# Attention and two MoE layers: transposes ahead of a product's last quarter, gate buffers for raw weights, sums behind j9

## The chip, the cores and the metric

The kernel runs on one core of a Trainium2 chip. The metric is device time in microseconds, from the first to the last instruction with the launch around it; the time of a kernel is the median of its runs.

## What is computed

Three layers, one after the other, on a batch of 4 with 8 heads, 576 positions and head dimension 64. All inputs and outputs are float32.

```python
scores = scale * np.matmul(q, k.transpose(0, 1, 3, 2))
bias = np.maximum(x @ w1 + b1, 0.0) @ w2      # x: log distances, 576 x 576
scores = scores + bias.transpose(2, 0, 1)[None, :, :, :]
attn = softmax(scores)
x = np.matmul(attn, v)                        # -> 2304 tokens x 512

h = x @ w_in                                  # first MoE: 512 -> 1024
e = np.exp(h - h.max(-1)); sm = e / (e.sum(-1) + 1e-09)
solu = h * sm
ln = (solu - mean) / np.sqrt(var + 1e-06) * g_ln
x = ln @ w_out                                # 1024 -> 512

gate = 1.0 / (1.0 + np.exp(-(x @ w_gate)))    # second MoE: 512 -> 1536
val = x @ w_val
out = gate * val @ w_out                      # 1536 -> 512
```

## The kernel before

Weights arrive as 64-bit floats, which the kernel reads as pairs of 32-bit words and decodes (`decode`, L184 to L199): two operations on ACT (L191, L192) and two on DVE (L193, L195) per pair of 128-row blocks. Every matrix operand is then split into a high and a low float16 part, and a product is the sum of three matmuls (high x high, high x low, low x high).

**Attention** runs in 72 ticks. A tick computes the scores of a block (`a_qk`, PE, L560 and L565, tile `score`), its softmax on DVE and ACT, a split into float16, a DMA transpose on SP's queue (L608, `pt`), and four ticks later the product with the values (L627, `xps`). K, V and Q arrive by DMA and are transposed on PE (`ktp` L258, `qtp` L297).

**First MoE.** It works by tiles of 128 tokens, 18 of them, as side work in the ticks: `moe_items` (L894) yields small pieces, three of which run in a tick. For tile i these are: `m_g1`, the first product, in four quarters of six matmuls (L773, PSUM tile `hps`, whose eviction with the row maximum is DVE's L784); `m_ew1`, exponential and product; `m_ew2`, mean and variance, ending in POOL's L807, which writes `e`; `m_ew3`, eight PE transposes of `e` (L816, `ltp`), each half of them copied out by ACT (L818) and DVE (L819) into `lt`; `m_g2`, the second product in four parts of 24 matmuls (L830, `x2ps`), which read `lt`, evicted by L835 and L836. `hps`, `ltp` and `x2ps` rotate through the PSUM banks of the pool `ps_m`: three buffers and, in the ticks, a fourth single bank that the class `Turns` (L91) puts at every fourth place. About 13 tiles are done within the attention; the rest follow, with `hps` in the ring `s_ps`.

**Weights of the second MoE.** 18 pairs of 1 MB each (two loads of 512 KB) are loaded by SP through `load_pair` (L1062 to L1071) into the tile `wraw`, for which there are two buffers, one from the end of attention and one from slightly later on; a load waits until the decode of the pair two before is done. ACT's L1148 squares the result for the column scales. `w2_split` (L702 to L706) then scales and splits it: a scaling (L704 on POOL or L702 on ACT, tile `w2tmp`), a copy (L705 on ACT) and the low part (L706 on POOL or DVE).

**Second MoE.** There are five groups of tiles (4, 2, 4, 4, 4). Groups 0 and 1 use `gate_val`: for each of 12 column blocks j, 24 matmuls (L1383) into one of the two buffers of `s_ps`, evicted by ACT's sigmoid (L1388, `fr`), DVE's product (L1389, `fr`) and `split_gv` (L1252 on ACT, L1253 on DVE) into the ring `gv` (two buffers). `second_out` (L1413, `ops`; L1417, `ob`) multiplies by w_out. Groups 2 to 4 use seven products of sums in place of eight (L1347, `prod`); the sums of weights and inputs come from `w2_sums` (six calls of 14 adds, the adds at L1271, tiles `fs` and `w2s`) and `x2_sums` (18 adds per group).

**What sets the order.** The program is written once; a scheduler places each instruction on its engine's queue by dependences and priority. In the attention ticks PE's order is that of the program. Each engine then runs its queue in order. `issue_after` makes a piece wait until a named instruction has issued: the sums of group 2 wait for `glob["so"]`, the last instruction of the scales of w_out.

Of the kernel before, what the change touches and what calls it, by code (L numbers as in the profile page):

```python
# [11 lines left out]
I32 = mybir.dt.int32  # L12
# [78 lines left out]
class Turns:  # L91


    def __init__(self, *pools):
        self.pools, self.n = list(pools), -1

    def tile(self, *a, **kw):
        self.n += 1
# [4 lines left out]
def attn_moe_kernel(  # L103
# [10 lines left out]
    def enter(stack, name, bufs=1, side="left", space=None):  # L114
        kw = {} if space is None else {"space": space}
        if space is None:
            kw["reuse_waits"] = "tile"
            kw["side"] = side
        return stack.enter_context(tc.tile_pool(name=name, bufs=bufs, **kw))
# [9 lines left out]
    att = ctx.enter_context(ExitStack())  # L129

    pss = ctx.enter_context(ExitStack())
    ps_m = Turns(*[enter(pss, "ps_m", 3, space=PSUM)] * 3)
    ps_v = enter(pss, "ps_v", 1, space=PSUM)
    psa = ctx.enter_context(ExitStack())
    ps_s = enter(psa, "ps_b0", 2, space=PSUM)
# [761 lines left out]
    def moe_items():  # L897
        for i in range(19):
            if i < 18:
                for n in range(2):  # L900
                    for half in range(2):
                        yield ready[i] + LAG_PV + LAG_X + 1, (lambda i=i, n=n, half=half: m_g1(i, n, half))
                yield 0, (lambda i=i: m_ew1(i))
            if i >= 1:
                yield 0, (lambda i=i: m_ew3(i - 1))
            if i < 18:
                yield 0, (lambda i=i: m_ew2(i))
            if i >= 1:
                for dc in range(4):
                    yield 0, (lambda i=i, dc=dc: m_g2(i - 1, dc))  # L910
# [149 lines left out]
    w2raw, loads = {}, []  # L1060

    def load_pair(mat, jc, cc):  # L1062
        raw = w2r_p.tile([128, 2, 512, 2], I32, name="wraw", tag="wraw")
        r0 = 256 * cc + (512 * jc if mat == 2 else 0)
        src = (w_gate, w_val, w_out2)[mat]
        cols = slice(0, DM) if mat == 2 else slice(512 * jc, 512 * jc + 512)
        for c in range(2):
            with tc.issue_after(loads[-1].ins):
                loads.append(sp.dma_start(out=raw[:, c].rearrange("p f t -> p (f t)"),
                                          in_=src[r0 + 128 * c:r0 + 128 * c + 128, cols].bitcast(I32)))  # L1070
        return raw  # L1071
# [3 lines left out]
    for t in range(nticks + LAG_PV + LAG_X + 1):  # L1075
        if not own and "open" in done:
            own.append(in_order.enter_context(tc.manual_schedule(engines={mybir.EngineType.PE})))
        with tc.high_priority(PRIO):
            for f in at.get(t, []):
                f()  # L1080
        for u in range(t, t + 3):
            if u < nticks:
                for tt in {0: (), 1: (2, 3), "M": (4,)}[ticks[u][1]]:
                    until(("bias", tt))
                load_bias(ticks[u])
        with tc.high_priority(PRIO):
            if t < nticks:
                a_qk(t)
                a_soft(t)
            if 0 <= t - 1 < nticks:  # L1090
                a_split(t - 1)
            if 0 <= t - LAG_PV - LAG_X < nticks:
                a_x(t - LAG_PV - LAG_X)
        if t % 2 == 0 and 2 <= t < 16:
            with tc.issue_after(trs[t - 1].ins):
                for n in (0, 1) if t == 2 else (t // 2,):
                    store0(n % 2, n // 2)
        for n in range(NB if "s" in glob else NB0):
            side_step(t)
            if n == 0:  # L1100
                with tc.high_priority(PRIO):
                    for f in late.get(t, []):
                        f()
        with tc.high_priority(PRIO):
            if 0 <= t - LAG_PV < nticks:
                a_pv(t - LAG_PV)
            if 0 <= t - LAG_PV - LAG_X < nticks:
                a_xt(t - LAG_PV - LAG_X)
        if t == nticks:
            w2r_p = Turns(enter(glob["s"], "w2e", 1))  # L1110
            loads.append(trs[nticks - 1])
            w2raw[0, 0, 0] = load_pair(0, 0, 0)
    in_order.close()
# [9 lines left out]
    grow("fr", 2, ctx)  # L1123
    d2 = ctx.enter_context(ExitStack())
    w2t_p = enter(d2, "w2t", 2, "right")
    w2r_p.pools.append(enter(d2, "w2r", 1, "right"))
    w2d_p = enter(d2, "w2d", 1, "right")
    w2f = [w2_p.tile([128, 12, 512], F32, name=f"w2f{i}") for i in range(3)]
    w2h16 = [w.bitcast(F16).rearrange("p a (l f) -> p a l f", l=2) for w in w2f]
# [106 lines left out]
        load_x2(0)  # L1236
    glob["s"].close()
    m1.close()
    w2r_p.pools[0] = enter(d2, "w2r2", 1, "right")
    grow("xb", 1, ctx, "left")  # L1240
    grow("gv", 2, ctx, "left")
    grow("fr", 3, ctx, "left")
# [7 lines left out]
    def split_gv(y, gv, js, t0, w):  # L1250
        hi, lo = (gv[:, l, js, t0:t0 + w] for l in range(2))
        act.activation(out=hi, in_=y, func=ACTF.Copy)  # L1252
        dve.tensor_tensor(out=lo, in0=y, in1=hi, op=ALU.subtract)  # L1253

    def half_w(mat, jc, kh, fh):

# [111 lines left out]
    def gate_val(g, n, xx, gvs, js):  # L1368
        nn = 128 * n
        for j in js:  # L1370
# [16 lines left out]
            sg = f32t().rearrange("p j q -> p (j q)")[:, 0:nn]  # L1387
            act.activation(out=sg, in_=prods[0], func=ACTF.Sigmoid, scale=sw[:, j // 4, W_CG:W_CG + 1])  # L1388
            dve.scalar_tensor_tensor(out=sg, in0=prods[1], scalar=2.0 ** -14, in1=sg, op0=ALU.mult, op1=ALU.mult)  # L1389
            split_gv(sg, gv, jj, 0, nn)  # L1390

    def gate_val7(n, xs_, gvs, jcs=range(3)):
        nn = 64 * n
# [50 lines left out]
    with tc.issue_after(glob["so"].ins):  # L1444
        for jc in range(3):
            for mat in range(2):
                w2_sums(mat, jc)
        xs_ = x2_sums(2)
    fring[0] = "fr"
    second_out(1, sizes[1], gvs1)  # L1450
    pss.close()
# [80 lines left out]
```

## Time and profile before

| | |
|---|---|
| median of 3 runs | 1060.28 us (1060.22 to 1061.12) |
| profiled execution, its own time | 1060.07 us |
| its span, first to last instruction | 1058.3 us |
| PE busy | 891.4 us (84%) |
| DVE busy | 732.9 us (69%) |
| ACT busy | 645.0 us (61%) |
| POOL busy | 385.6 us (36%) |
| chain that ended last | PE 35%, DVE 7%, ACT 4%, issue 3% |

The profiled execution has 1.8 us around its span, and it is 0.2 us under the median. Busy shares are means over stages: the attention with most of the first MoE lasts to about 568 us, the rest of the first MoE and the decoding of the second MoE's weights to about 690, and from there the second MoE's matmuls.

### The profile page before, as it was taken

To read this page: it belongs to the slowest core of one execution; us is meant where nothing else is said; L and a number is where in the kernel's file an instruction comes from. 1 tells how busy PE (TensorE), PEld (TensorE's weight loads), DVE (VectorE), ACT (ScalarE), POOL (GpSimd) and SP (SyncE) were. 2 spreads that over 40 slices of the span, in tenths; PEclk is the share of its full clock that TensorE was granted. 3 is DMA by queue.
4 is the path that set the end of the run, shared out by engine and by line. 5 is a ranking of instruction groups with operands and counts; after the bars stand their busy time and mean duration, and the time that the engine had idled before them with its cause. 6 is when DMAs were issued, how large, how long until landed. Compare 5 with 4: busy or idle time off the path is not lost.

```text
span 1058.3 us, 23827 instructions
## 1 busy us (share of the span) xinstructions
PE 891.4 (84%) x9572; PEld 632.2 (60%) x9572; DVE 732.9 (69%) x1471; ACT 645.0 (61%) x1275; POOL 385.6 (36%) x362
## 2 busy tenths in 40 slices
PE   2656563669888889999999888988999999999998
PEld 2634342446656657666766566435578857866873
DVE  6878986696676776576664897699935763871760
ACT  4788877576877788877974888774333322332231
POOL 3357555374666556554550483351000000000000
PEclk9557776679998899999999899898999999999999
DMA  7977999799999699999965655300010010001001
GB/s 224 296 217 192 250 240 242 179 218 215 218 207 197 159 207 189 197 210 201 173 123 163 210 173 200 126 16 35 31 46 16 1 61 21 1 11 31 2 1 40
DMA packets 256575, 146.54 MB, mean 138 GB/s; under 512 B 215376, under 2 KB 230992, under 8 KB 256464
## 3 DMA queue, kind: packets, MB, share of 16 engines
q1 hardware_dynamic: 253168, 141.86, 56.1%
q0 software_dynamic: 2048, 1.58, 0.6%
q8 instruction: 75, 1.23, 0.5%
q10 hardware_dynamic: 1248, 1.57, 0.4%
q14 instruction: 36, 0.29, 0.1%
HBM read 82.46 MB, written 20.05 MB: 97 GB/s over the span
## 4 chain that ended last, share of the span: by engine, by line
PE 35%; DVE 7%; ACT 4%; issue 3%; POOL 1%; DMA 1%; SPq 0%; ACTq 0%; POOLq 0%; DVEq 0%
PE prod L1347 16%; PE ops L1413 12%; PE s_ps L1383 3%; DVE fs L1271 2%; PE x2ps L830 2%; DMA wraw<-in_moe_w_out_dram 1%; PE hps L773 1%; POOL w2tmp L704 1%; DVE w2f L195 1%; DVE w2f L193 1%; ACT wraw L192 1%; DVE w2s L1271 1%; ACT w2junk L1148 1%; PE xps L627 1%; ACT w2f L191 1%
## 5 line engine op out<-in xcount | busy, mean ns | idle before, releaser
L603 POOL TENSOR_TENSOR p<-p,p 128x1024 f16<-128x1024 f32 x72 | 156.7, 2177 | 138.3 <-ACT p L602 93.5
L1271 DVE TENSOR_TENSOR fr<-prod,fr 128x512 f32<-128x512 f32 x126 | 85.0, 687 | 94.3 <-PE prod L1347 92.6
L1413 PE MATMUL ops<-w2f,gv 128*128 128x512 f16 x648 | 142.3, 379 | 0.0
L591 ACT ACTIVATE p<-p,m,sc 128x576 f32<-128x576 f32 x144 | 124.0, 862 | 2.5
L830 PE MATMUL x2ps<-lt,w1f 128*128 128x128 f16 x1728 | 110.2, 223 | 10.0 <-DVE lt L819 7.4
L627 PE MATMUL xps<-gk,pt 128*128 128x64 f16 (+1 forms) x2240 | 85.7, 201 | 35.8 <-DMA pt<-p 29.4
L1383 PE MATMUL s_ps<-xb,w2f 128*128 128x512 f16 (+1 forms) x576 | 103.6, 339 | 14.1 <-DVE fr L1389 11.5
L584 DVE CUSTOM_DVE_ANT_0 p<-score,gk 128x576 f32<-128x576 f32 x144 | 102.9, 751 | 17.7 <-PE score L565 15.0
L830 PEld LDWEIGHTS <-w1f 128*128 128x128 f16 x1728 | 104.2, 100 | 14.4 <-issue 11.6
L627 PEld LDWEIGHTS <-pt 128*128 128x128 f16 (+1 forms) x2240 | 80.5, 106 | 46.3 <-DMA pt<-p 37.3
L1413 PEld LDWEIGHTS <-gv 128*128 128x128 f16 x648 | 63.4, 98 | 73.9
L463 PEld LDWEIGHTS <-mask 128*128 128x128 f16 (+1 forms) x1312 | 64.0, 120 | 48.9 <-issue 26.5
L1347 PEld LDWEIGHTS <-w2f 128*128 128x128 f16 x864 | 84.5, 98 | 11.8 <-issue 1.1
L1383 PEld LDWEIGHTS <-w2f 128*128 128x128 f16 x576 | 58.0, 101 | 55.6 <-issue 13.4
L1252 ACT ACTIVATE gv<-fr 128x512 f16<-128x512 f32 (+1 forms) x60 | 34.7, 585 | 84.2 <-DVE fr L1403 70.4
L560 PE MATMUL score<-gk,qt 64*128 64x512 f16 (+1 forms) x480 | 67.6, 418 | 14.6 <-DVE m L584 11.3
L773 PE MATMUL hps<-w1f,xt 128*128 128x512 f16 x312 | 75.0, 388 | 4.2 <-DVE mm L784 3.6
L463 PE MATMUL bp<-rhs,mask 128*128 128x64 f16 (+1 forms) x960 | 49.2, 222 | 24.2 <-DVE gk L489 6.7
L602 ACT ACTIVATE p<-p 128x1152 f16<-128x1152 f32 x54 | 62.7, 1160 | 11.2 <-DMA pt<-p 8.8
L1347 PEld LDWEIGHTS <-w2s 128*128 128x128 f16 x648 | 63.4, 98 | 7.3
L589 ACT ACTIVATE m<-m,sc 128x1 f32<-128x1 f32 x144 | 39.5, 286 | 44.3 <-DVE m L584 44.2
L773 PEld LDWEIGHTS <-xt 128*128 128x128 f16 x384 | 37.1, 100 | 45.4 <-issue 9.4
(199 smaller groups left out, 1740.7 us busy)
## 6 DMA issues: line engine op xcount, KB each, us to landing
gk<-bias_d SPq DMA_DIRECT2D x24, 576.0 KB
wraw<-in_moe_w_out_dram SPq DMA_DIRECT2D x20, 512.0 KB
wraw<-in_moe_w_gate_dram SPq DMA_DIRECT2D x12, 512.0 KB
wraw<-in_moe_w_val_dram SPq DMA_DIRECT2D x12, 512.0 KB
sraw<-in_q_dram SPq DMA_DIRECT2D x12, 384.0 KB
sraw<-in_k_dram SPq DMA_DIRECT2D x12, 384.0 KB
sraw<-in_v_dram SPq DMA_DIRECT2D x12, 384.0 KB
bias_d<-gk SPq DMA_DIRECT2D x8, 576.0 KB
```

Source lines behind the costliest of these rows:

```text
L463: pe.matmul(big[0:np_, jj // 8, o:o + 64], lhsT, rhs[i].rearrange("p c h g -> p (c h g)"), start=(i == 0), stop=(i == 1),)
L560: pe.matmul(score[p0:p1, 1024 * hh:1024 * hh + 512], qt[rows, nr * ql + r, p0:p1], KT[bb, hp][rows, 640 * kl:640 * kl + 512], start=(m == ...
L584: dve.tensor_tensor_reduce(out=pp[:, hh], in0=score[:, 960 * hh:960 * hh + S], in1=bi, scale=1.0, scalar=-3.0e38, op0=ALU.add, op1=ALU.max ...
L591: act.activation(out=pp[:, hh], in_=pp[:, hh], func=ACTF.Exp, bias=m[:, 2 + hh:3 + hh], scale=col(C), accum_out=sm[:, c + hh:c + hh + 1])
L603: pool.tensor_tensor(out=p16[:, :, 640:1152], in0=view(pp, 0, [[640, 2], [1, 512]]), in1=view(p16, 0, [[1280, 2], [1, 512]]), op=ALU.subtract)
L627: pe.matmul(o, a, b_, start=(n == 0), stop=(n == len(seq) - 1))
L773: pe.matmul(h, xt[:, xl, kk, off:off + 128], win16[:, 2 * kk + n, wl], start=(kk == 0 and xl == 0 and wl == 0), stop=(kk == 3 and xl == 1),)
L830: pe.matmul(ps[:, dc], wout16[:, f, wl, 128 * dc:128 * dc + 128], lt[:, ll, f], start=(n == 0), stop=(n == 23))
L1271: dve.tensor_tensor(out=out_, in0=a, in1=b, op=op)
L1347: pe.matmul(p[:, jf, 0:nn], w(wl, kk, jf), x(xl, kk), start=(m == 0), stop=(m == 5))
L1383: pe.matmul(ps[:, 0:n], w[:, 4 * (j // 4) + c, wl, o:o + 128], xx[:, 0:n, c, xl, :], start=(m == 0), stop=(m == 11))
L1413: pe.matmul(ps, gvs[j // 4][:, gl, j % 4, 128 * tt:128 * tt + 128], w2h16[2][:, j, wl], start=(m == 0), stop=(m == 35))
```

## The change

It has four parts. The turns over the PSUM banks start at another number, so other tiles get the fourth bank. Pairs 1, 2, 5 and 6 of the raw weights are loaded into the two `gv` buffers, which gate_val does not use yet; the others take `wraw`'s two. The sums wait for the low part (L1253's instruction) of j9 of group 0, and `x2_sums(2)` follows the first third of `w2_sums`. In the first MoE, `m_ew3` of the tile before stands ahead of the last quarter of `m_g1`, and `m_ew2` directly behind `m_ew1`.

```diff
 class Turns:
-    def __init__(self, *pools):
-        self.pools, self.n = list(pools), -1
+    def __init__(self, pool):
+        self.pools, self.n = [pool] * 3, 0
...
-    ps_m = Turns(*[enter(pss, "ps_m", 3, space=PSUM)] * 3)
+    ps_m = Turns(enter(pss, "ps_m", 3, space=PSUM))
...
                     for half in range(2):
+                        if n == half == 1 and i >= 1:
+                            yield 0, (lambda i=i: m_ew3(i - 1))
                         yield ready[i] + LAG_PV + LAG_X + 1, (lambda i=i, n=n, half=half: m_g1(i, n, half))
                 yield 0, (lambda i=i: m_ew1(i))
-            if i >= 1:
+                yield 0, (lambda i=i: m_ew2(i))
+            else:
                 yield 0, (lambda i=i: m_ew3(i - 1))
-            if i < 18:
-                yield 0, (lambda i=i: m_ew2(i))
...
     def load_pair(mat, jc, cc):
-        raw = w2r_p.tile([128, 2, 512, 2], I32, name="wraw", tag="wraw")
+        n = len(loads) // 2
+        if n in (1, 2, 5, 6):
+            raw = ring("gv", [128, 2, 512, 2], I32)
+        else:
+            raw = w2r_p[n in (3, 7) or (n > 8 and n % 2)].tile([128, 2, 512, 2], I32, name="wraw", tag="wraw")
...
     def split_gv(y, gv, js, t0, w):
...
-        dve.tensor_tensor(out=lo, in0=y, in1=hi, op=ALU.subtract)
+        return dve.tensor_tensor(out=lo, in0=y, in1=hi, op=ALU.subtract)
...
-            split_gv(sg, gv, jj, 0, nn)
+            low_ = split_gv(sg, gv, jj, 0, nn)
+            if (g, j) == (0, 9):
+                glob["so"] = low_
...
         for jc in range(3):
             for mat in range(2):
                 w2_sums(mat, jc)
-        xs_ = x2_sums(2)
+            if jc == 0:
+                xs_ = x2_sums(2)
```

The order of instructions shows it at three places. The first is PE in the attention, at a tile whose second product follows in the same tick (`ltp` are the transposes, `hps` the first product of the next tile, `x2ps` the second product). Before, the rows were:

```order
L565 LDWEIGHTS qt
L565 MATMUL score<-gk,qt 128x2x64
L816 MATMUL ltp<-id_sb,e 128x128 x8
L297 MATMUL qtp<-id_sb,qraw 128x128 x2
L830 LDWEIGHTS w1f_111
L830 MATMUL x2ps<-lt,w1f_111 128x128
```

and the change has, at that tile:

```order
L773 LDWEIGHTS xt
L773 MATMUL hps<-w1f_110,xt 128x512
L816 MATMUL ltp<-id_sb,e 128x128 x8
L773 LDWEIGHTS xt
L773 MATMUL hps<-w1f_110,xt 128x512
L773 LDWEIGHTS xt
```

The transposes (x8) stood behind the last `hps` and the `score` of the tick, two `qtp` ahead of the first `x2ps`; they now stand between two quarters of `hps`, and the six matmuls of the last quarter, a tick's `xps` and `score` come between them and `x2ps`.

The second is DVE at the end of the decoding (w2f_9631 is w_out's tile, L193 and L195 decode one pair of it; the `fr` are those of j2 and j3, on whose bank j4 waits). Before, three pairs of w_out were decoded ahead of these two `fr` and the next stood behind them:

```order
L195 SCALAR_TENSOR_TENSOR w2f_9631<-wraw,w2f_9631 128x1024
L836 SCALAR_TENSOR_TENSOR x_10612<-x2ps,x_10612 128x4x128
L1389 SCALAR_TENSOR_TENSOR fr<-s_ps,fr 128x512 x2
L706 TENSOR_TENSOR w2f_9629<-w2tmp,w2f_9629 128x512
L193 SCALAR_TENSOR_TENSOR w2f_9631<-w2f_9631,wraw 128x1024
L1253 TENSOR_TENSOR gv<-fr,gv 128x512
L195 SCALAR_TENSOR_TENSOR w2f_9631<-wraw,w2f_9631 128x1024
L1253 TENSOR_TENSOR gv<-fr,gv 128x512
L706 TENSOR_TENSOR w2f_9629<-w2tmp,w2f_9629 128x512
L193 SCALAR_TENSOR_TENSOR w2f_9631<-w2f_9631,wraw 128x1024
L195 SCALAR_TENSOR_TENSOR w2f_9631<-wraw,w2f_9631 128x1024
L1389 SCALAR_TENSOR_TENSOR fr<-s_ps,fr 128x512
```

and now:

```order
L193 SCALAR_TENSOR_TENSOR w2f_9631<-w2f_9631,wraw 128x1024
L195 SCALAR_TENSOR_TENSOR w2f_9631<-wraw,w2f_9631 128x1024
L162 TENSOR_REDUCE acc<-w2st 128x1 x2
L836 SCALAR_TENSOR_TENSOR x_10612<-x2ps,x_10612 128x4x128
L169 TENSOR_SCALAR cl<-tot 128x3
L1258 TENSOR_TENSOR gv<-fr,gv 128x512
L171 TENSOR_SCALAR ci<-cl 128x3
L1258 TENSOR_TENSOR gv<-fr,gv 128x512
L172 TENSOR_SCALAR ci<-ci 128x3
L1394 SCALAR_TENSOR_TENSOR fr<-s_ps,fr 128x512
L173 TENSOR_SCALAR sw<-ci 128x3
L1394 SCALAR_TENSOR_TENSOR fr<-s_ps,fr 128x512
```

All six pairs are ahead of the two `fr` (L1394 in the changed file), with the first steps of w_out's scales (L169 to L173). On SP's queue, the twelve loads of w_out now stand in one row, and the load of `xb` for group 1 behind them.

The third is DVE at the start of the sums (`gv` is the low part's eviction; L1271 is L1276 in the changed file, L1253 is L1258). Before, the sums began with the eviction of j8 still to come:

```order
L1253 TENSOR_TENSOR gv<-fr,gv 128x512
L1177 SCALAR_TENSOR_TENSOR sw<-sw,sc 128x1 x3
L1179 SCALAR_TENSOR_TENSOR sc<-sc 128x1
L1271 TENSOR_TENSOR fs<-w2f_9629 128x512 x3
L1271 TENSOR_TENSOR fs<-fs 128x512
L1271 TENSOR_TENSOR fs<-w2f_9629 128x512
L1389 SCALAR_TENSOR_TENSOR fr<-s_ps,fr 128x512
L1271 TENSOR_TENSOR fs<-fs 128x512
L1271 TENSOR_TENSOR w2s_11685<-fs,w2s_11685 128x512
L1271 TENSOR_TENSOR fs<-fs,w2f_9629 128x512
L1271 TENSOR_TENSOR fs<-w2f_9630 128x512
L1253 TENSOR_TENSOR gv<-fr,gv 128x512
```

and now:

```order
L1394 SCALAR_TENSOR_TENSOR fr<-s_ps,fr 128x512
L1258 TENSOR_TENSOR gv<-fr,gv 128x512
L1394 SCALAR_TENSOR_TENSOR fr<-s_ps,fr 128x512
L1258 TENSOR_TENSOR gv<-fr,gv 128x512
L1394 SCALAR_TENSOR_TENSOR fr<-s_ps,fr 128x512
L1258 TENSOR_TENSOR gv<-fr,gv 128x512
L1276 TENSOR_TENSOR fs<-w2f_9629 128x512 x3
L1276 TENSOR_TENSOR fs<-fs 128x512
L1276 TENSOR_TENSOR fs<-w2f_9629 128x512
L1276 TENSOR_TENSOR w2s_11685<-fs,w2s_11685 128x512
L1276 TENSOR_TENSOR fs<-fs 128x512
L1394 SCALAR_TENSOR_TENSOR fr<-s_ps,fr 128x512
```

The scales that stood directly ahead of the sums are further up, and the `fr` and `gv` of j8 and j9 are ahead of the first sum.

## Rows read from the trace of the kernel before

**Rows 1.** Busy time by stretch: us from:to, length, each engine, PEclk, DMA share, GB/s.

```profile
125.00:150.00 25.00, 14.00 (x211) 11.16 (x211) 19.14 (x46) 18.44 (x38) 15.20 (x15) 0.66 1.09 251
600.00:625.00 25.00, 24.10 (x239) 17.12 (x238) 22.18 (x45) 21.87 (x33) 18.22 (x15) 0.93 0.56 183
700.00:725.00 25.00, 18.10 (x86) 9.24 (x84) 25.00 (x28) 14.84 (x27) 13.12 (x9) 0.86 0.12 42
750.00:775.00 25.00, 25.00 (x175) 16.86 (x174) 21.93 (x39) 11.04 (x21) 0.00 (x0) 1.00 0.06 22
```

**Rows 2.** Chain of waits, 690 to 800: start us, us, what.

```profile
692.16 2.42 DVE fs L1271 x4
...
729.60 0.34 DVE fr L1389
...
729.99 2.78 PE s_ps L1383 x24
...
795.24 0.69 ACT ob L1417
...
795.98 4.09 PE prod L1347 x36
```

**Rows 3.** Waits of PE, 590 to 800: total us, times, longest us.

```profile
PE s_ps L1383 <- DVE fr L1389: 11.5, 3, 4.7
```

**Rows 4.** PE's timeline: start, us, line, operation, count, [idle before <-releaser].

```profile
604.46 2.75 PE L773 MATMUL s_ps<-w1f,xt 128*128 128x512 f16 x12 [0.52 <-DVE mm L784]
...
663.14 23.16 PE L1383 MATMUL s_ps<-xb,w2f 128*128 128x512 f16 x95 [4.64 <-DVE fr L1389]
...
706.08 5.34 PE L1383 MATMUL s_ps<-xb,w2f 128*128 128x512 f16 x24 [2.16 <-DVE fr L1389]
...
718.10 5.07 PE L1383 MATMUL s_ps<-xb,w2f 128*128 128x256 f16 x24 [4.74 <-DVE fr L1389]
```

**Rows 5.** Waits of PE, 250 to 568.

```profile
PE x2ps L830 <- DVE lt L819: 7.0, 8, 1.6
PE ktp L258 <- DMA kv<-in_k_dram: 5.7, 3, 2.9
...
PE ltp L816 <- DVE mm L784: 3.1, 3, 1.8
...
PE x2ps L830 <- ACT lt L818: 1.8, 3, 0.8
```

**Rows 6.** Waits of SP's queue, 555 to 690, then of ACT, 560 to 690.

```profile
SPq L1069 <- DVE w2f L195: 76.5, 15, 7.3
...
ACT w2f L191 <- DMA wraw<-in_moe_w_out_dram: 6.9, 3, 3.0
...
ACT wraw L192 <- DMA wraw<-in_moe_w_gate_dram: 5.0, 1, 5.0
ACT w2f L191 <- DMA wraw<-in_moe_w_gate_dram: 4.1, 1, 4.1
```

**Rows 7.** Groups by line, 560 to 700: busy us, mean ns of one.

```profile
L191 ACT ACTIVATE w2f<-wraw 128x1024 f32<-128x1024 f32 x18 | 20.6, 1144 | 11.7 <-DMA wraw<-in_moe_w_out_dram 6.9 <-DMA wraw<-in_moe_w_gate_dram 4.1 <-DMA wraw<-in_moe_w_val_dram 0.5
...
L192 ACT ACTIVATE wraw<-wraw 128x1024 int32<-128x1024 uint16 x18 | 20.5, 1140 | 5.0 <-DMA wraw<-in_moe_w_gate_dram 5.0
...
L1148 ACT ACTIVATE w2junk<-w2f 128x1024 bf16<-128x1024 f32 x12 | 12.6, 1050 | 3.2 <-DVE w2f L195 3.2
```

**Rows 8.** Timelines of DVE and of POOL, at 706.

```profile
706.55 1.64 DVE L1271 TENSOR_TENSOR fs<-w2f 128x512 f32<-128x512 f16 x1
...
706.08 1.56 POOL L706 TENSOR_TENSOR w2f<-w2tmp,w2f 128x512 f16<-128x512 f32 x1 [3.61 <-ACT w2f L705]
```

**Rows 9.** The page's costliest groups: busy us, mean ns of one | idle before, releaser.

```profile
L1271 DVE TENSOR_TENSOR fr<-prod,fr 128x512 f32<-128x512 f32 x126 | 85.0, 687 | 94.3 <-PE prod L1347 92.6
```

**Rows 10.** Waits of PE, 60 to 250.

```profile
PE xps L627 <- DMA pt<-p: 28.9, 12, 5.2
PE ktp L258 <- DMA kv<-in_k_dram: 9.6, 3, 4.7
```

More of the change, by code (lines that the diff above doesn't have):

```diff
@@ L1109, in attn_moe_kernel @@
         if t == nticks:
-            w2r_p = Turns(enter(glob["s"], "w2e", 1))
+            w2r_p = [enter(glob["s"], "w2e", 1)]
             loads.append(trs[nticks - 1])
@@ L1125, in attn_moe_kernel @@
     w2t_p = enter(d2, "w2t", 2, "right")
-    w2r_p.pools.append(enter(d2, "w2r", 1, "right"))
+    w2r_p.append(enter(d2, "w2r", 1, "right"))
     w2d_p = enter(d2, "w2d", 1, "right")
@@ L1238, in attn_moe_kernel @@
     m1.close()
-    w2r_p.pools[0] = enter(d2, "w2r2", 1, "right")
+    w2r_p[0] = enter(d2, "w2r2", 1, "right")
     grow("xb", 1, ctx, "left")
```

## Prediction

> **What bounds the kernel now.** I read the busy time by stretches first, because the change touches three places with different limits [rows 1]. The columns to look at are PE's busy time, PEclk and the DMA share. From 125 to 150 us PE works 14.00 of 25 us, with the 16 DMA engines full (share 1.09): loads and DMA transposes set that stage. From 600 on PE is nearly full, 24.10 of 25, except where the second MoE starts: in 700:725 it works 18.10 us at clock 0.86 while DVE works 25.00. So DVE leads there, and PE follows.
>
> The chain of waits says the same [rows 2]: from 692.16 to 729.60 its pieces are DVE's, nearly all the sums of L1271, with a `fr` (L1389) between them; at 729.99 it goes over to PE and stays there, and 795.98 is the first seven-product matmul, behind a 0.69 us wait for ACT's `ob`. What follows is dense matmul work that the change leaves alone. So I look for time only ahead of 795.98.
>
> PE's own waits give its size [rows 3]: after 590 the bank evictions `fr` cost it 11.5 us in 3 waits. The timeline [rows 4] places them: 4.64 us before 663.14 (behind the decoding), 2.16 before 706.08 and 4.74 before 718.10 (both behind sums). In the attention stage [rows 5] the second product of the first MoE (`x2ps`) waits for `lt` 7.0 and 1.8 us in eleven waits.
>
> **Transposes a quarter earlier.** No instruction is added or removed: eight transposes, their copies on ACT (L818) and DVE (L819), and the normalisation pass (ew2) move. The eleven waits, 7.0 + 1.8 = 8.8 us, are PE waiting for copies whose transposes it has just done. Now six matmuls of L773 lie between (twelve took 2.75 us [rows 4], so about 1.4 us), and often a whole tick's `xps` and `score` too. The longest such wait is 1.6 us [rows 5], so nearly all 8.8 can go. What is late next: the copies now stand on ACT and DVE ahead of the last quarter's bank evictions (L784), for which `ltp` waits 3.1 us already [rows 5], and PE reaches the k loads (`ktp`, 5.7 us) sooner. Ends: 0 (all of it turns into those waits) and -11.9 (8.8, and the 3.1 of `ltp` too). I take **-5**, a little over half, since the waits on L784 show that this ring is short of banks.
>
> **Four load buffers.** SP's queue waits 76.5 us in 15 waits for the last decoding step (L195) to free a buffer, and ACT waits 6.9 + 4.1 + 5.0 = 16.0 us for the loads that therefore come late [rows 6]. With four buffers for the first eight pairs those 16.0 us can go. But the order puts something in their place: all six pairs of w_out are now decoded, with the squares, ahead of `fr` of j2 and j3, where three of them came after it. Three pairs more on ACT ahead of that point are 3 x (1.144 + 1.140 + 1.050) = 10.0 us [rows 7]; with a fourth square and the readings of the sums of squares that go with them, some 12 us. So the start of j4, now 663.14 [rows 4], moves by +12 less what comes back of 16.0. Ends: +12 (nothing comes back) and -4 (all). I take half, **+4**; the same ACT also waits for POOL and DVE, which more buffers don't shorten.
>
> **Sums after j9.** In the order of before the sums stand on DVE from j8's `fr` on, now from j10's. About seven adds lie between two `fr` either way; what differs is what they meet. Some adds take 1.64 us, beside a POOL split of 1.56 us [rows 8], others 0.6 (four in 2.42 us at 692.16 [rows 2]). With four slow ones in seven a j costs DVE 4 x 1.64 + 3 x 0.6 + 1.3 (`fr` and `gv`) = 9.7 us, and PE needs 5.34 for its 24 matmuls [rows 4]: hence the waits of 2.16 and 4.74. With none it is 7 x 0.6 + 1.3 = 5.5, and PE, which has `ops` of about a microsecond to put between, need not wait. The splits follow the scales of w_out; those come before j4 in the changed order, and the sums start some 35 us after j4 does (six j's of 5.3 and a few `ops`), so the splits should be over. From 663.14 to 795.98 are 132.84 us. Out of these go 2.16 + 4.74 = 6.9, and the slow clock behind the second wait: 24 matmuls of 256 columns took 5.07 us at 718.10 (1.2 GHz) and 2.78 at 729.99 (2.4 GHz) [rows 2, 4], 2.3 us. The slow start at 663.14 stays, since PE will idle before j4 again. 6.9 + 2.3 = **-9**; ends -10 (`ob` too) and 0 (the splits are not over).
>
> The later sums need cover: 84 adds of w2_sums and 18 of x2_sums at 0.6 are 61 us on DVE, with some 11 us of `fr` and `gv` between them, so they end 35 + 61 + 11 = 107 us after j4. Their first reader is the matmul now at 795.98, then 124 us after j4: 17 us of cover; 8 at 0.687, the mean of adds of the same size later on [rows 9]. Were it gone, each us of lateness would be one at that matmul.
>
> A rule bears on the 1.64. The Trainium skill (SBUF — State Buffer, "Who interferes with whom") says that GpSimd and VectorE share one pair of SBUF ports as an exclusive lock. By it an add costs 0.6 or a whole split more, whatever the order of the sums, and the 9 us come back only if POOL is done; if the 1.64 had another cause that moves along, nothing of the 9 would. The trace's two durations speak for the lock.
>
> **Banks renumbered.** It costs no instruction, but the scheduler's order from the first ticks on is another: k's transposes come at other places, and SP's loads too. PE's waits there are for DMA, 28.9 us for `pt` in 12 and 9.6 us for k in 3, the longest 5.2 [rows 10]. No row tells what a reordering is worth: by the nearest, one such wait more or less, **0**, ends -5 and +5; DMA is full either way.
>
> **Sum.** -5 + 4 - 9 + 0 = -10 against the profiled execution, 1060.07 us (span 1058.3 and 1.8 around it): 1050. The median of the runs is 0.2 above it, so **1050.3 us**.
>
> **Rivals.** First, *decoding sets the pace*: ACT and DVE have more before j4 and nothing comes back, +12. The sums' 9 and the transposes' 5 leave -2: 1058. For it: DVE and ACT are busy about 22 of 25 us in 600:625 [rows 1]. Against: 16.0 us of ACT's idle time there has the loads' name on it.
>
> Second, *the sums come too late*: if one add in three still met a split, the waits of 6.9 and the slow clock would stay (1059), and 102 adds would take 34 x 1.64 + 68 x 0.6 = 97 us and end 35 + 97 + 11 = 143 us after j4, where the first reader then stands 133 after it: up to 10 us more, 1069, if those read first are among the last. Against: POOL is idle in 750:775 [rows 1], as its splits are done by then.
>
> Third, *the first MoE gives nothing*, for the L784 banks: 1055.
>
> Fourth, *clean*: the loads give back all 16.0 us, the transposes 8.8: -8.8 - 4 - 9 = -22, or 1038; where one of the two stays at a half, 1042 to 1046.
>
> Fifth, on the other side, **slower**: the new order of the first ticks. That stage has DMA full at a share of 1.09 and PE at clock 0.66 [rows 1], and one transpose queued behind two loads holds a tick. Three more waits like the longest (5.2 for `pt`, 4.7 for k [rows 10]), about 15 us, decide against the -10 from the second such wait on: 1065. For it: PE's order differs from its first rows. Against: bytes and packets are the same.
>
> The change may also not act in part: the gate buffers wait for attention's end before they take a pair, so the first load into one may start no earlier than now. That is the first rival's time.
>
> **Numbers.** Chances: the forecast 0.45, decoding 0.14, late sums 0.07, first MoE nothing 0.09, clean 0.11, slower order 0.14. A measurement of this kernel can tell about 0.2%, 2 us, from no change. Decoding lies at that edge: 0.07 of it is faster, 0.05 within, 0.02 slower. Late sums are 0.03, 0.02 and 0.02; of the slower order, 0.02 with only one such wait is within. Faster: 0.45 + 0.09 + 0.11 + 0.07 + 0.03 = 0.75. Within: 0.05 + 0.02 + 0.02 = 0.09. Slower: 0.12 + 0.02 + 0.02 = 0.16. The likeliest case alone spans 1045 to 1055. The range takes in the first and third rivals, the clean case with one half, and the near part of the other two: 1042 to 1062.
>
> **What would show it.** Right: `x2ps` waits for `lt` under 3 us; SP's wait for L195 far under 76.5; no wait of `s_ps` on `fr` after j4 begins; that stretch down to about 123 us; the sums at about 0.6 us each and done before the first seven-product matmul. Wrong: j4 starting more than 8 us later against the end of attention; a wait of that matmul for `w2s`; ticks before 250 us that end over 5 us later than now.

## The result, and the profile after

The changed kernel takes 1049.59 us (median of 4 runs, 1048.68 to 1050.72) against 1060.70 for the kernel before on the same chip: a ratio of 0.9888, 95% interval 0.9857 to 0.9919. The forecast was 1050.3. The profiled execution took 1050.22 us; the page gives its span, the busy times of its engines and PE's granted clock:

```profile
span 1048.4 us, 23815 instructions
...
PE 886.8 (85%) x9568; PEld 627.2 (60%) x9572; DVE 720.8 (69%) x1471; ACT 645.8 (62%) x1275; POOL 386.5 (37%) x362
...
PEclk9756676668999999999999999899999999999999
```

The span was 1058.3, so 9.9 us are gone. Where they went is read with four marks that both traces have: the end of tick 23's and of tick 71's softmax (the second L584 of the tick on DVE), the start of j4, and the first seven-product matmul. The table holds the time from mark to mark in the two profiled executions, beside the term of the prediction for that stretch.

| stretch | before | after | difference | forecast |
|---|---|---|---|---|
| start to tick 23 | 265.3 | 259.5 | -5.8 | 0 |
| tick 23 to tick 71 | 284.7 | 280.9 | -3.8 | -5 |
| tick 71 to j4 | 113.1 | 122.4 | +9.3 | +4 |
| j4 to the first seven-product matmul | 132.9 | 123.1 | -9.8 | -9 |
| from there to the end | 262.3 | 262.5 | +0.2 | 0 |

The total is the forecast's, the terms are not: the first is 6 us better, the third 5 us worse, and the two errors cancel. So the sum alone would have taught the wrong thing. Each stretch is read from one execution, and executions of one kernel differ by several us (the 19 of the kernel before that ran beside e11 and e12 took 1056.6 to 1063.9); a stretch tells something only where several kernels agree on it, and the table of the experiments is there for that.

The stretches again, with PE's busy time first, and PEclk, DMA share and GB/s last (the rows that answer to [rows 1]):

```profile
125.00:150.00 25.00, 16.66 (x264) 12.83 (x263) 22.73 (x53) 21.51 (x48) 13.90 (x12) 0.79 1.02 256
600.00:625.00 25.00, 20.02 (x181) 12.98 (x180) 19.95 (x38) 18.66 (x29) 17.65 (x15) 1.00 0.46 155
650.00:675.00 25.00, 19.01 (x140) 10.62 (x138) 17.01 (x33) 20.97 (x36) 13.35 (x13) 0.86 0.19 67
700.00:725.00 25.00, 25.00 (x165) 15.98 (x164) 24.82 (x44) 10.89 (x21) 0.00 (x0) 1.00 0.14 43
```

In 700:725 PE works 25.00 us at full clock where it had 18.10 at 0.86; in 600:625 it works 20.02, and had 24.10. PE's timeline around j4 shows both sides (for [rows 4]):

```profile
659.81 0.38 PE L164 MATMUL tot<-acc,ones_sb 128*128 128x3 f32 x2 [3.35 <-DVE acc L162]
662.84 13.15 PE L1388 MATMUL s_ps<-xb,w2f 128*128 128x512 f16 x48 [2.64 <-DVE fr L1394]
...
709.93 2.78 PE L1388 MATMUL s_ps<-xb,w2f 128*128 128x256 f16 x24
...
785.91 1.47 PE L1352 MATMUL prod<-xb,w2f 128*128 128x256 f16 x12 [0.78 <-ACT ob L1424]
```

j4 starts at 662.84 behind two waits, 3.35 and 2.64 us. After it PE has no gap until the 0.78 before the first seven-product matmul: the waits of 2.16 and 4.74 are gone, and the 256-column matmuls at 709.93 take 2.78 us where those at 718.10 took 5.07.

In the attention, PE's waits from 250 to 568 were (for [rows 5]):

```profile
PE ktp L258 <- DVE lt L819: 5.0, 2, 3.7
PE ltp L816 <- DVE qt L300: 4.1, 1, 4.1
...
PE qtp L297 <- DVE lt L819: 2.4, 1, 2.4
...
PE ktp L258 <- DMA kv<-in_k_dram: 1.9, 2, 0.9
```

No wait of `x2ps` for `lt` is left there. What stands in its place are waits of `ktp` and `qtp` for `lt`, 5.0 and 2.4 us, and one of `ltp` for `qt`, 4.1 us: 11.5 us for the 8.8 that went. All three are tiles of `ps_m`, and each waits for a bank that DVE has still to empty. The k loads' 5.7 us are now 1.9. In all, PE's waits from tick 23 to tick 71 are not fewer, 28.0 us after 26.4. What fell is PE's busy time, by 5.3 us, at a mean granted clock of 0.98 where it was 0.96 (before, then the change):

```profile
265.30:550.00 284.70, 258.09 (x3611) 186.79 (x3612) 195.71 (x483) 227.12 (x503) 166.93 (x149) 0.96 0.95 189
...
259.50:540.40 280.90, 252.82 (x3601) 182.70 (x3600) 190.02 (x484) 225.32 (x499) 167.69 (x149) 0.98 0.97 188
```

Ahead of tick 23, the waits for DMA fell from 28.9 and 9.6 us [rows 10] to 16.2 and 3.7:

```profile
PE xps L627 <- DMA pt<-p: 16.2, 9, 3.4
...
PE ktp L258 <- DMA kv<-in_k_dram: 3.7, 3, 1.8
```

SP's queue and ACT in the decoding stage (for [rows 6]):

```profile
SPq L1074 <- DVE w2f L195: 70.9, 14, 14.0
...
ACT wraw L192 <- DMA wraw<-in_moe_w_gate_dram: 4.5, 1, 4.5
ACT w2f L191 <- DMA wraw<-in_moe_w_out_dram: 2.3, 2, 1.4
```

ACT's waits for loads fell from 16.0 us to 6.8, those of SP's queue for a buffer from 76.5 to 70.9.

### The profile page after: what moved, and what is told of

It is laid out like the page before. It is cut to its first block, busy times and chain, and to the rows that moved or that the text cites. A ratio compares the mean times of both kernels' runs of the same rounds, so it can differ in the third digit from the quotient of the medians.

```text
span 1048.4 us, 23815 instructions
## 1 busy us (share of the span) xinstructions
PE 886.8 (85%) x9568; PEld 627.2 (60%) x9572; DVE 720.8 (69%) x1471; ACT 645.8 (62%) x1275; POOL 386.5 (37%) x362
## 5 line engine op out<-in xcount | busy, mean ns | idle before, releaser
L603 POOL TENSOR_TENSOR p<-p,p 128x1024 f16<-128x1024 f32 x72 | 160.6, 2230 | 128.3 <-ACT p L602 88.9
L1276 DVE TENSOR_TENSOR fr<-prod,fr 128x512 f32<-128x512 f32 x126 | 85.1, 688 | 92.3 <-PE prod L1352 90.6
L830 PE MATMUL x2ps<-lt,w1f 128*128 128x128 f16 x1728 | 106.9, 222 | 4.4 <-DVE x L836 2.1
L584 DVE CUSTOM_DVE_ANT_0 p<-score,gk 128x576 f32<-128x576 f32 x144 | 102.8, 750 | 9.3 <-PE score L565 5.7
L1388 PE MATMUL s_ps<-xb,w2f 128*128 128x512 f16 (+1 forms) x576 | 100.9, 332 | 6.9 <-DVE fr L1394 2.6
L830 PEld LDWEIGHTS <-w1f 128*128 128x128 f16 x1728 | 101.9, 100 | 4.8 <-DVE x L836 2.2
L463 PEld LDWEIGHTS <-mask 128*128 128x128 f16 (+1 forms) x1312 | 61.0, 117 | 55.0 <-issue 30.5
```

The costliest lines, as they stand in the source:

```text
L463: pe.matmul(big[0:np_, jj // 8, o:o + 64], lhsT, rhs[i].rearrange("p c h g -> p (c h g)"), start=(i == 0), stop=(i == 1),)
L584: dve.tensor_tensor_reduce(out=pp[:, hh], in0=score[:, 960 * hh:960 * hh + S], in1=bi, scale=1.0, scalar=-3.0e38, op0=ALU.add, op1=ALU.max ...
L603: pool.tensor_tensor(out=p16[:, :, 640:1152], in0=view(pp, 0, [[640, 2], [1, 512]]), in1=view(p16, 0, [[1280, 2], [1, 512]]), op=ALU.subtract)
L830: pe.matmul(ps[:, dc], wout16[:, f, wl, 128 * dc:128 * dc + 128], lt[:, ll, f], start=(n == 0), stop=(n == 23))
L1276: dve.tensor_tensor(out=out_, in0=a, in1=b, op=op)
L1388: pe.matmul(ps[:, 0:n], w[:, 4 * (j // 4) + c, wl, o:o + 128], xx[:, 0:n, c, xl, :], start=(m == 0), stop=(m == 11))
```

## The experiments

Twelve kernels ran. The table gives their medians, the ratio to the kernel before on the same chip with its interval (its median there was 1060.3 to 1061.0), and the stretches of the table above in the profiled execution of each. The column "pairs" counts, in the order of DVE's instructions, the decoded pairs that stand ahead of j2's and j3's evictions.

| kernel | us | ratio, 95% interval | to tick 23 | 23 to 71 | 71 to j4 | pairs | j4 to seven products |
|---|---|---|---|---|---|---|---|
| before | 1060.3 | 1 | 265.3 | 284.7 | 113.1 | 15 | 132.9 |
| the change | 1049.6 | 0.989 (0.986 to 0.992) | 259.5 | 280.9 | 122.4 | 18 | 123.1 |
| e1 sums alone | 1056.1 | 0.996 (0.994 to 0.998) | 268.2 | 283.8 | 112.4 | 15 | 127.6 |
| e2 all but sums | 1060.1 | 0.999 (0.998 to 1.001) | 261.0 | 278.2 | 124.2 | 18 | 132.4 |
| e3 banks alone | 1067.5 | 1.005 (1.003 to 1.007) | 259.7 | 290.1 | 119.1 | 16 | 133.5 |
| e4 all but loads | 1049.3 | 0.989 (0.986 to 0.992) | 259.3 | 277.9 | 123.3 | 16 | 123.5 |
| e5 loads alone | 1071.6 | 1.010 (1.007 to 1.013) | 266.9 | 283.8 | 121.9 | 18 | 133.1 |
| e6 constant 3 | 1048.4 | 0.987 (0.985 to 0.990) | 260.1 | 278.3 | 115.9 | 14 | 132.3 |
| e7 constant 5 | 1047.9 | 0.987 (0.984 to 0.991) | 258.7 | 278.3 | 122.4 | 16 | 123.3 |
| e8 low parts on DVE | 1050.8 | 0.990 (0.987 to 0.993) | 258.1 | 282.5 | 123.1 | 18 | 123.2 |
| e9 held behind j3 | 1044.0 | 0.985 (0.983 to 0.987) | 263.3 | 278.2 | 117.1 | 12 | 123.1 |
| e10 held, POOL | 1050.7 | 0.991 (0.988 to 0.994) | 259.2 | 278.0 | 118.9 | 12 | 129.5 |
| e11 banks, transposes | 1058.7 | 0.999 (0.997 to 1.000) | 261.2 | 278.6 | 122.9 | 16 | 133.3 |
| e12 all but transposes | 1059.0 | 0.998 (0.996 to 0.999) | 260.5 | 289.5 | 122.1 | 18 | 122.8 |

The last stretch is 262.3 to 262.5 us in all of them.

### The sums, with and without the rest (e1, e2)

The first takes the kernel before and moves the sums alone; the second takes the change and leaves them where they were.

```diff
-            split_gv(sg, gv, jj, 0, nn)
+            low_ = split_gv(sg, gv, jj, 0, nn)
+            if (g, j) == (0, 9):
+                glob["so"] = low_
...
-        xs_ = x2_sums(2)
+            if jc == 0:
+                xs_ = x2_sums(2)
```

> The kernel before with the sums moved behind j9 (and x2_sums forward), nothing else. Theory A (the four parts add): everything up to the start of j4 stays, j4 near 663; from there to the first seven-product matmul 123 us instead of 132.8; time -9 to -10, 1051. Rival (the sums gain only because w_out's scales and POOL's splits also come earlier in the full change): the splits still run beside the first sums, some adds stay at 1.64 us, waits of s_ps on fr of 2 us or more stay after j4, gain 0 to -5.

> The full change with the sums left where they were (behind w_out's scales). Theory A: j4 starts as in the change, near 663; adds of 1.64 us beside POOL's splits come back, waits of s_ps on fr of some 7 us, and the stretch from j4 to the first seven-product matmul is 132 us; time 1059. Rival (the splits come earlier in the full change, so that the place of the sums is indifferent): that stretch stays at 123 to 126, time 1049 to 1052.

Alone, the sums' move gives 5.3 us of the 9.8 in the stretch behind j4 and 0.42% of the time, some 4.5 us. This lies in the rival's range (0 to -5), and a wait on `fr` of 2.62 us stays after j4, as the rival said. In the full change it gives 10.5 us (1060.1 against 1049.6), as theory A had it. What differs is POOL. With the sums alone, POOL's last split ends at 715.2, 51 us after j4, and the sums start at 703.1; six adds take over 1.2 us, each beside a split. Timelines of DVE, then of POOL, in e1:

```profile
710.38 1.65 DVE L1271 TENSOR_TENSOR w2s<-fs,w2s 128x512 f16<-128x512 f32 x1
711.95 1.65 DVE L1271 TENSOR_TENSOR fs<-fs,w2f 128x512 f32<-128x512 f32 x1
...
709.79 1.68 POOL L706 TENSOR_TENSOR w2f<-w2tmp,w2f 128x512 f16<-128x512 f32 x1 [2.41 <-ACT w2f L705]
711.88 1.17 POOL L706 TENSOR_TENSOR w2f<-w2tmp,w2f 128x512 f16<-128x512 f32 x1 [0.40 <-ACT w2f L705]
```

In the full change the order puts the scales of w_out ahead of j4, so the splits end at 687.9, 25 us after j4, and the first add starts at 700.76. No add takes over 1.2 us. POOL's last splits there:

```profile
677.77 1.16 POOL L706 TENSOR_TENSOR w2f<-w2tmp,w2f 128x512 f16<-128x512 f32 x1 [0.65 <-ACT w2f L705]
...
685.43 2.43 POOL L706 TENSOR_TENSOR w2f<-w2tmp,w2f 128x512 f16<-128x512 f32 x2 [0.49 <-ACT w2f L705]
```

With the sums in their old place (e2), nine adds take over 1.2 us, each beside a split. PE's waits, one of the adds, and POOL's splits:

```profile
PE s_ps L1388 <- DVE fr L1394: 8.2, 3, 4.2
...
675.59 1.68 DVE L1276 TENSOR_TENSOR fs<-fs,w2f 128x512 f32<-128x512 f32 x1
...
675.55 4.29 POOL L706 TENSOR_TENSOR w2f<-w2tmp,w2f 128x512 f16<-128x512 f32 x3 [0.55 <-ACT w2f L705]
685.08 8.02 POOL L706 TENSOR_TENSOR w2f<-w2tmp,w2f 128x512 f16<-128x512 f32 x5 [5.24 <-ACT w2f L705]
697.92 7.94 POOL L706 TENSOR_TENSOR w2f<-w2tmp,w2f 128x512 f16<-128x512 f32 x2 [4.82 <-ACT w2f L705]
```

### The ports: the splits taken off POOL (e8)

```diff
-                act if mat == 2 else None, dve if mat < 2 and c % 2 else None)
+                act if mat == 2 else None, dve if mat == 2 or c % 2 else None)
```

> The full change with the sums where they were before, and w_out's low parts (L706) on DVE instead of POOL, so that POOL runs no two-input operation beside the sums. Theory of the shared ports: no add takes over 1.2 us (9 did with the sums in their old place), though 12 low parts of 0.6 us come to DVE; the waits of s_ps on fr fall from 5.6 us to 0 to 3; time 1053 to 1058 against 1060. Rival (the slow adds come from something else, say from ACT's or PE's accesses at that time): the same number of adds near 1.6 us, and a later time, 1063 or more.

The sums start at 668.8, where e2 has them, five microseconds after j4. DVE has 12 more operations to do, and the stretch behind j4 falls from 132.4 to 123.2 us. No add is slow; PE's waits on `fr` are the one ahead of j4 (2.6), where e2 has 8.2 with that one; and 24 of the adds, which e2's view has at a mean of 816 ns, are at 692:

```profile
PE s_ps L1388 <- DVE fr L1394: 2.6, 1, 2.6
...
L1276 DVE TENSOR_TENSOR fs<-w2f 128x512 f32<-128x512 f16 x24 | 16.1, 692 | 0.0
```

So POOL's splits are what makes adds slow, and the rival falls: with w_out's splits gone from POOL, which then does nothing beside the sums, their place is indifferent. That the ports are what the two engines share is not shown by this run. The time is even under the 1053 to 1058 that had been expected. Moving the sums was one way to part the two; moving 12 small operations is another, and gives the same time (1050.8 against 1049.6, with intervals that overlap).

### The banks and the transposes (e3, e11, e12)

```diff
-        self.pools, self.n = list(pools), -1
+        self.pools, self.n = [pool] * 3, 0
```

The third run has this alone (w2r_p keeps its old turns), the eleventh with the moved transposes, the twelfth is the change without them. The moved transposes were not tried with the banks as they were.

> The kernel before with the banks renumbered, nothing else. Theory A: the first ticks end about 6 us earlier, as in the change (tick 23 near 259.5 instead of 265.3), the rest as before: j4 near 657, time 1054. Rival (the early ticks of the change are earlier through the loads or the transposes, or by chance of one execution): tick 23 stays within 2 us of 265, time 1060.

> The kernel before with the banks renumbered and the transposes moved, old loads and old sums. The run with the banks alone needed 290 us from tick 23 to tick 71, the runs with both 278 to 281. Theory A3 (the transposes' gain is 9 to 12 us, not 5, because the renumbered banks alone cost 5 there): tick 71 near 538, 16 pairs ahead of j2's and j3's evictions, so j4 near 661, then the old 132 to 133 us with waits behind the sums; time 1055 to 1059, against 1067.5 for the banks alone. Rival (the difference in those ticks came from the order that sums or loads leave further up): tick 71 near 548, time 1064 to 1068.

> The full change without the transposes' move. Theory A3: tick 71 near 549, waits of x2ps for lt of 8 us or more as in the kernel before, all 18 pairs ahead, so j4 117 to 122 us later, near 668; from there 123 us; time 1054 to 1059, that is 5 to 9 above the change. Rival (the transposes gain nothing in the full change, for the stage up to j4 takes back what the attention gives): time 1048 to 1051.

In e3 tick 23 ends at 259.7, as theory A expected, so the early gain is the banks'. It is no chance of one execution: ten other kernels with the new banks have it between 258.1 and 263.3, and with the old ones it is 265.3, 266.9 and 268.2. But the time is 1067.5, seven over before: theory A was wrong from tick 23 on. There the banks alone cost 5.4 us (290.1 against 284.7): `x2ps` waits longer for `lt`, and `ktp` for its loads:

```profile
PE x2ps L838 <- DVE lt L827: 10.6, 8, 3.0
PE ktp L266 <- DMA kv<-in_k_dram: 8.6, 3, 3.7
```

Before, these were 7.0 and 5.7 us [rows 5]. Then 16 pairs instead of 15 stand ahead of j2's and j3's evictions: 6.0 us more to j4.

The eleventh run answers what the transposes are worth with these banks: 290.1 becomes 278.6. The `x2ps` waits go, and waits on the banks come, of which the longest is:

```profile
PE ktp L266 <- DVE lt L827: 5.1, 2, 3.7
```

The twelfth says the same from the other end: without them, 289.5 us instead of 280.9, and its waits are those of e3:

```profile
PE x2ps L830 <- DVE lt L819: 11.0, 8, 3.0
PE ktp L258 <- DMA kv<-in_k_dram: 8.7, 3, 4.1
```

So with these banks the transposes take 11.5 us (e3 to e11) and 8.6 us (e12 to the change) out of those ticks. Of PE's waits there, 32.7 us in e3 and in e12, 24.7 are left in e11 and 28.0 in the change. In e11 8.8 us of that reach the end (1058.7 against 1067.5), in e12 9.4 (1059.0 against 1049.6).

### The load buffers (e4, e5)

```diff
-        n = len(loads) // 2
-        if n in (1, 2, 5, 6):
-            raw = ring("gv", [128, 2, 512, 2], I32)
-        else:
-            raw = w2r_p[n in (3, 7) or (n > 8 and n % 2)].tile([128, 2, 512, 2], I32, name="wraw", tag="wraw")
+        raw = w2r_p.tile([128, 2, 512, 2], I32, name="wraw", tag="wraw")
```

> The full change with the raw weights in two buffers as before. Theory A (the decoding of all of w_out ahead of j2's and j3's evictions costs what the attention gained): the last tick ends near 540 as in the change, j4 starts 113 us later as in the kernel before, near 653.5, and the time is 1040, under the change's. Rival (something that does not move with the attention paces the stage up to j4, such as the loads): j4 stays near 663, time 1049; or the loads in two buffers hold it up further, 1053.

> The kernel before with the four load buffers, nothing else. Theory A2 (j4 starts when the last pair that stands on DVE ahead of j2's and j3's evictions is decoded, and the number of pairs ahead decides: 15 before, 16 with the banks, all 18 with the loads): pairs are decoded faster, the 18th some 118 us after the last tick instead of 132, but all 18 are ahead, so j4 starts about 122 us after the last tick instead of 113: time +8 to +9, near 1069. Rival (four buffers give back what they take, as I predicted by halves): j4 113 to 117 us after the last tick, time 1060 to 1064.

Without the buffers the time is 1049.3: they are worth nothing here. Theory A falls with it, for j4 still starts 123.3 us after the last tick, though the loads are the old ones; and the rival in its first form holds as far as the time goes (j4 at 660.5). Neither said why, so I formed another (A2): the start of j4 is the end of the last decoded pair that the order puts ahead of j2's and j3's evictions. After the last tick the pairs are done at these times:

| kernel | pair 14 | pair 15 | pair 16 | pair 18 | ahead | j4 |
|---|---|---|---|---|---|---|
| before | 108.3 | 111.9 | 119.3 | 132.0 | 15 | 113.1 |
| e3 banks alone | 107.3 | 112.5 | 118.5 | 128.8 | 16 | 119.1 |
| e4 all but loads | 108.9 | 114.3 | 122.7 | 132.6 | 16 | 123.3 |
| the change | 95.4 | 102.2 | 106.8 | 117.5 | 18 | 122.4 |
| e5 loads alone | 90.9 | 99.2 | 102.7 | 115.5 | 18 | 121.9 |

With two buffers j4 follows its pair by 0.6 to 1.2 us, and there the rule fits. With four the 18th pair comes 15 us sooner than in before, and all of it is spent: the order waits for three pairs more. Behind the 18th come 5 us more (6.4 in e5), the square, the scales' matmul on PE, then `x`, `gv` and the two `fr`. DVE in the change, with the last pair's L195, the last reading of the squares (L162), the two `fr` (L1394), and the first sum:

```profile
656.71 1.22 DVE L195 SCALAR_TENSOR_TENSOR w2f<-wraw,w2f 128x1024 int32<-128x1024 int32 x1
...
659.60 0.15 DVE L162 TENSOR_REDUCE acc<-w2st 128x1 f32<-128x2 f32 x1 [1.60 <-ACT w2junk L1153]
...
662.10 0.68 DVE L1394 SCALAR_TENSOR_TENSOR fr<-s_ps,fr 128x512 f32<-128x512 f32 x1
...
662.76 0.69 DVE L1394 SCALAR_TENSOR_TENSOR fr<-s_ps,fr 128x512 f32<-128x512 f32 x1
...
700.76 1.89 DVE L1276 TENSOR_TENSOR fs<-w2f 128x512 f32<-128x512 f16 x3
```

j4 follows the first of the two `fr`, that of j2, by 0.06 us; j3's it does not wait for. In the change the chain that ended last does run through the last pair: its load, its steps on ACT and its squares, the eviction of the first MoE's last tile, the `fr`, j4:

```profile
653.17 1.16 ACT w2f L191
...
656.22 1.76 ACT w2junk L1153 x4
...
659.57 0.49 ACT x L835
```

But a second path ends close beside it. PE's timeline, before and then in the change, has the last matmuls of the first MoE's last tile:

```profile
652.81 4.41 PE L830 MATMUL x2ps<-lt,w1f 128*128 128x128 f16 x76
...
651.66 4.80 PE L830 MATMUL x2ps<-lt,w1f 128*128 128x128 f16 x83
```

They end 107.3 us after the last tick before and 116.0 in the change. So 8.7 of the 9.3 us are lost ahead of that point, where PE's waits are 16.8 us and were 10.6, and from there to j4 it takes 6.4 us for 5.9.

e5 was expected at 1069 by A2 and came at 1071.6, with j4 at 121.9 against 122: the buffers alone make the kernel slower by 1%, and the halves that I had predicted for them don't hold.

### Fewer pairs ahead (e6, e7, e9, e10)

Two runs hand out the weights' work more slowly among the first MoE's last tiles:

```diff
-W2B = 10
+W2B = 3
```

> The full change with the weights' work handed out more slowly between the last tiles of the first MoE (constant 3 in place of 10), which leaves 14 pairs ahead of j2's and j3's evictions and the scales of w_out behind j7 on PE. Theory A2: j4 starts when pair 14 is decoded, near 95 to 105 us after the last tick instead of 122; time 1033 to 1042 if w_out's splits still come in time for the first ops, some of it lost in waits of ops otherwise. Rival (the first MoE's last tiles, not the pairs, hold j4 back): j4 stays 115 us or more after the last tick, time 1045 to 1050.

> As the run before with the constant at 5: 16 pairs ahead. Theory A2: j4 near 107 to 112 us after the last tick (the change decoded pair 16 at 106.8), time 1036 to 1042. Rival: as before, 1045 to 1050.

The pair rule holds for j4 and the times fail. In e6 pair 14 is done at 113.4 and j4 starts at 115.9; in e7 (constant 5) pair 16 is done at 119.9 and j4 starts at 122.4. DVE in e7 shows pair 16's L195 and the two `fr`, 2.9 us apart:

```profile
655.72 1.21 DVE L195 SCALAR_TENSOR_TENSOR w2f<-wraw,w2f 128x1024 int32<-128x1024 int32 x1
...
658.66 1.28 DVE L1394 SCALAR_TENSOR_TENSOR fr<-s_ps,fr 128x512 f32<-128x512 f32 x2
```

But with the work handed out later the pairs are decoded later: pair 11 at 92.1 us in e7 and 74.9 in the change. In e6 the splits, too, come later (until 708.4), six adds are slow beside them, and the stretch behind j4 is 132.3 again. Against the change, neither differs by more than the intervals. These two runs also tell what held the last tile of the first MoE: with the constant at 10, 5 and 3 PE ends it 116.0, 111.5 and 106.9 us after the last tick, and waits 16.8, 14.2 and 9.8 us until then. The weights' work that is handed out among these tiles is what delays them.

So the next kernels leave the handing out nearly as it was (constant 8), put w_out's pairs last, hold DVE's two steps of them behind j3's low part, and hand out no such work in j0 to j3; the first of them has w_out's low parts on DVE as in e8:

```diff
-W2B = 10
+W2B = 8
...
-        decode(w, raw.rearrange("p c f t -> p (c f) t"), dve)
+        if mat == 2 and "f3" in glob:
+            with tc.issue_after(glob["f3"].ins):
+                decode(w, raw.rearrange("p c f t -> p (c f) t"), dve)
+        else:
+            decode(w, raw.rearrange("p c f t -> p (c f) t"), dve)
...
-            take(5 if j < 8 else 7)
+            take(0 if j < 4 else 7)
...
+            if (g, j) == (0, 3):
+                glob["f3"] = low_
```

> The full change, with DVE's two decoding steps of all six pairs of w_out held behind j3's low part (12 pairs ahead of j2's and j3's evictions instead of 18), the scales of w_out on PE behind j9, and w_out's low parts on DVE as in the run before. Theory A2 (the pairs that stand ahead of these evictions set j4's start): j4 100 to 110 us after the last tick instead of 122, near 640 to 648; if w_out's splits are ready when the first ops need them, time 1030 to 1040. Rival (ACT's work in that stage is the bound, whatever the order on DVE): j4 115 us or more after the last tick, or what it gains comes back as waits of ops for w_out's splits; time 1045 to 1050.

> As the run before, but w_out's low parts on POOL as in the change. Theory A2 with the shared ports: j4 as there; POOL's splits now run some 20 us later against j4, so the first sums meet them again: 4 to 10 adds over 1.2 us, waits of s_ps on fr of 3 to 8 us, time 3 to 8 us above the run before. Rival (the ports matter little): the two within 2 us.

e9 is the fastest of all, 1044.0 us, 5.6 under the change; the intervals of the ratio (0.983 to 0.987, and 0.986 to 0.992) overlap only at their ends. It is no 1030 to 1040: its 12 pairs are done 82.9 us after the last tick, and j4 starts at 117.1. The pairs no longer decide; all that this run alters is worth 5.3 us of that stretch (122.4 to 117.1). Timelines of PE, then of DVE:

```profile
649.96 5.47 PE L830 MATMUL x2ps<-lt,w1f 128*128 128x128 f16 x95
...
658.65 6.61 PE L1391 MATMUL s_ps<-xb,w2f 128*128 128x512 f16 x22 [2.57 <-DVE fr L1397]
...
656.10 0.69 DVE L836 SCALAR_TENSOR_TENSOR x<-x2ps,x 128x512 f16<-128x512 f32 x1 [1.80 <-ACT x L835]
...
657.91 1.28 DVE L1397 SCALAR_TENSOR_TENSOR fr<-s_ps,fr 128x512 f32<-128x512 f32 x2
```

PE does the last tile's second product until 655.4, 113.9 us after the last tick; then come its eviction (L836), the low parts and `fr` of the j's before, and j4. So the rival had j4's place right (115 us or more) and its time nearly (1045 to 1050). That ACT's work is the bound, as it says, no run shows; what holds j4 back next is the first MoE's last tile.

e10 differs from e9 in the low parts alone, and nine adds are slow again, the stretch behind j4 is 129.5 instead of 123.1, and the time 6.7 us more, as expected. A wait on `fr` and one of `ops` on POOL's split itself are in PE's timeline:

```profile
712.10 4.32 PE L1391 MATMUL s_ps<-xb,w2f 128*128 128x256 f16 x24 [2.49 <-DVE fr L1397]
...
725.12 3.18 PE L1425 MATMUL ops<-w2f,gv 128*128 128x512 f16 x14 [1.20 <-POOL w2f L706]
```

## Why the prediction was right, and where it was not

**Transposes a quarter earlier, -5.** The stretch gave -3.8. The eleven waits went, as the step said, and waits on banks came in their place, as it also said, though not on L784's: 11.5 us on `lt` and `qt`. PE's waits in all did not fall there (28.0 us after 26.4), so the size came right in part by luck. With the new banks in both kernels the transposes give 8.6 to 11.5 us; the renumbered banks, which I costed at nothing there, cost 5.4. The term was right as the sum of two that I had not parted. What the transposes give with the old banks no run shows.

**Banks renumbered, 0 (ends -5 and +5).** The start gave -5.8, a little outside my ends, and e3 shows that it is this part alone. The reason that I named, DMA waits that the order moves about, is the right place: the waits for `pt` and for k are 18.6 us fewer in that stretch, of which 5.8 reach the time. Why this order is better was not settled. The fifth rival, a slower order of the first ticks, did not come about.

**Four load buffers, +4.** This is the step that failed. It gave +9.3, and the reason was further off than the size. I subtracted half of ACT's waits for loads, 8 us, from the 12 of three pairs more. ACT's waits did fall, by 9.2 us, and the decoding of all 18 pairs ended 14.5 us sooner after the last tick; none of that came off j4's start. The order puts all 18 pairs ahead of j4, and the weights' work stands among the first MoE's last tiles: PE ends the last of them 8.7 us later after the last tick, and the runs that hand out that work more slowly (e7, e6) take back 4.5 us and all of it. Behind that tile the 18th pair and its squares are on the chain. With the old loads the stage is as long (123.3), for 16 pairs stand ahead there, and each costs some 6 us. So the buffers cost 8.8 us of that stretch when put into the kernel before alone (e5), and taken out of the change they give nothing (e4). The sign that I had named came: j4 over 8 us later after attention's end; and one sign of being right did not, for SP's wait for L195 is 70.9 us and not far under 76.5. The first rival, "decoding sets the pace", is what happened in that stretch (+9.3, and I gave it +12); its total of 1058 did not come about, for the banks gave 5.8 at the start.

**Sums after j9, -9.** It gave -9.8, by the mechanism named: no wait on `fr` behind j4, full clock, 0.6 us an add, sums done in time (the first seven-product matmul waits for `ob` alone). Of the sums in the eight kernels that have slow ones, 66 adds take over 1.2 us, and each stands beside a POOL split; in the six kernels where the splits are over or gone (the change, e4, e7, e8, e9, e12) none does. The Trainium skill (SBUF — State Buffer, "Who interferes with whom") calls the shared pair of ports an exclusive lock. All 66 agree with it; that the ports are what is shared, these runs can't show. Not each add that overlaps a split is slow: seven in before are not, so the later of two seems to be the one that waits, which no run shows singly. The second rival needed POOL to be late; in e1 it is, and half of the gain is gone.

**Sum, -10.** It was -9.9, by two errors of 5.8 and 5.3 us of opposite sign. The range, 1042 to 1062, held it; that the total met the forecast within a microsecond is luck.

## What to carry to other kernels

When a scheduler writes the order, look up what the new order puts ahead of the instruction that PE waits for, and time that; here a faster supply was worth nothing, as the order then waited for more of it. Where VectorE's adds met GpSimd's splits, parting them in time and moving the smaller set to the other engine gave the same time, and the run with the smaller set moved shows whether that was the cause. And check a forecast by its stretches, not by its total.

## What had not been expected of the hardware

The slowing goes both ways. POOL's split takes 1.16 us with DVE quiet (at 677.77 in the change) and 1.56 beside single adds [rows 8]; where DVE had one add behind the other (e2), two of them took 7.94 us in all, at 697.92.
